# Queries sent with the head dimension outermost, and every other input sent tile by tile

## The chip, the cores and the metric

The kernel runs on one core of one Trainium2 chip. What is measured is the time of the whole program on the device, in microseconds (us); a kernel's time is the median of its runs. The layout in which inputs lie in device memory when the program starts is part of the kernel's own code: it prepares them on the host, and that is not in the time.

## The reference

Three stages follow each other on 8 x 576 = 4608 tokens with 512 features (8 heads of 64).

```python
kv  = einsum('bhsd,bhse->bhde', k, v)          # linear attention, 8 batches, 8 heads
out = einsum('bhsd,bhde->bhse', q, kv)
out = out / sqrt(mean(out*out, -1) + 1e-6) * g_norm
x   = out.transpose(0, 2, 1, 3).reshape(4608, 512)
xn  = x / sqrt(mean(x*x, -1) + 1e-6) * rms_g   # gated feed-forward, width 1536
g   = xn @ w_gate
x   = (g * sigmoid(g) * (xn @ w_val)) @ w_out
e   = argmax(x @ moe2_w_gate, 1)               # one of 8 experts for each token, width 1024
y   = gate * (relu(x @ w1[e]) @ w2[e])         # gate: softmax value of the chosen expert
```

q, k, v, w1 and w2 are float32; w_gate, w_val and w_out come as 64-bit floats, which the kernel narrows itself on ScalarE and VectorE. The large products split each operand in a high and a low part and run three passes.

## The kernel before, in words

The tokens are worked through in nine chunks of 512. A chunk c up to 7 holds 512 tokens of batch c, four to a partition; chunk 8 gathers the last 64 tokens of all eight batches. Chunks 0 to 3 run alone, chunk 4 runs alone with the attention of two batches beside it, and the pairs (4, 5) and (6, 7) run through a form with seven products instead of eight. After chunk 8 come the experts.

TensorE's stream is written by hand. In each chunk a loop over twelve blocks of the feed-forward width issues a gate product (`pg`), a value product (`pv`) and the products with w_out (`po`); between them the function `group` takes at most a step or two from a queue `aux`. The attention of batch c + 1 lies in that queue as a list of steps (`Attention.steps`, lines 797 to 845): between two steps stands an empty one, and the kinds of the steps say at which places of the pairs they are allowed. So an instruction of the attention stands in the stream where its step is taken, and each engine works in the order in which the code issues.

A batch's attention goes by pairs of heads (hp 0 to 3) in two halves of two pairs. `load` brings k, v and q of a pair; `load_left` the last 64 tokens of k and v; `load_last` those of q, two batches together. `column` copies k, and later q, so that the two heads of a pair stand beside each other (lines 679 to 683, on ScalarE; on VectorE for k of batch 0). `kv` multiplies k with v into a block diagonal `kvb`, filled by a copy on VectorE and one on ScalarE (lines 699, 700). `turn` transposes q on TensorE, four transposes for a pair, and ScalarE copies the result out of PSUM (lines 702 to 713). `av` multiplies the turned q with `kvb` and squares the result on ScalarE; GpSimd weighs the squares with g_norm, and VectorE sums both kinds (`squares`, `sums`). `finish`, `root` and `scale` normalise; `tstep` transposes the chunk into `xt`, with `comb` (rms_g times g_norm) as scale.

Batch 0 stands ahead of the loop, written out in lines 1466 to 1516. There 56 transposes of the identity into a tile that nobody reads (line 1505) run between the last `av` and the first `tstep`. The weights of the feed-forward pass through `Convert`: `load`, `rebias` (ScalarE), `narrow` (three passes on VectorE), `high` (ScalarE) and `low` (VectorE), four raw buffers in flight.

All loads named here are issued by SP, in program order; SP waits with a load until its buffer is free. k, v and q have two buffers each, the turned q (tag `qT`) and the column copies (tag `col`) as well.

Of the kernel before, what the change touches and what calls it, by code (L numbers as in the profile page):

```python
# [11 lines left out]
F32 = mybir.dt.float32  # L12
# [54 lines left out]
def attention_moe_kernel(ctx, tc, q, k, v, g_norm, w_gate, w_val, w_out, rms_g, wg2, w1, w2, out):  # L67
# [36 lines left out]
    wg2s = const([P, KD, E], F32, "wg2s")  # L104
    comb = const([P, KD], F32, "comb")
    gcol = const([P, 1], F32, "gcol")
    g2b = const([P, HD], F32, "g2b")
# [18 lines left out]

    def small_loads():
        nc.sync.dma_start(gcol[0:64, :], g_norm.rearrange("(e o) -> e o", o=1))
        nc.sync.dma_start(gcol[64:128, :], g_norm.rearrange("(e o) -> e o", o=1))
        with nc.allow_non_contiguous_dma(reason="one small vector"):  # L130
            nc.sync.dma_start(comb, rms_g.rearrange("(k p) -> p k", p=P))

    def late_loads():
        nc.sync.dma_start(wg2s, wg2.rearrange("(k p) e -> p k e", p=P))
# [39 lines left out]
    class Expert:  # L174
# [12 lines left out]
        def load(self, i):  # L187
            r = raw(f"re{self.nm}_{i}")
            e = self.ereg
            if i < 4:  # L190
                nc.sync.dma_start(
                    r.rearrange("p (k f) -> p k f", k=KD),
                    w1[ds(e, 1), :, i * 256 : i * 256 + 256].rearrange(
                        "o (k p) f -> p (o k) f", p=P
                    ),
                )
            else:
                a = (i - 4) * 256
                nc.sync.dma_start(
                    r.rearrange("p (a d) -> p a d", a=2),  # L200
                    w2[ds(e, 1), a : a + 256, :].rearrange("o (a p) d -> p (o a) d", p=P),
                )
            self.raws[i] = r
# [404 lines left out]
    wgt = dpool.tile([E, D], F32, name="wgt")  # L608
# [12 lines left out]
    class Attention:  # L621


        def __init__(self, b, ps):
            self.b, self.ps = b, ps
            self.n = 5 if b % 2 == 1 else 4
            self.t, self.col = {}, {}
            self.first, self.later = deque(), deque()
            self.qTs = deque()

        def load(self, *hps):
# [3 lines left out]
            for nm in "kvq":  # L635
                for hp in hps:
                    t = att.tile([P, 2, 4, HD], F32, tag=nm, bufs=2, name=f"{nm}{b}_{hp}")
                    nc.sync.dma_start(
                        t.rearrange("p h j d -> p h (j d)"),
                        {"k": k, "v": v, "q": q}[nm][b, 2 * hp : 2 * hp + 2, 0:512, :].rearrange(  # L640
                            "h (p j) d -> p h (j d)", j=4
                        ),
# [7 lines left out]
        def load_rest(self):  # L650

            self.t[2], self.t[3] = {}, {}
            for nm, src in (("k", k), ("v", v), ("q", q)):
                t = wpool.tile([P, 1024], F32R, tag="w", bufs=NSLOT, name=f"{nm}rest").bitcast(F32)
                nc.sync.dma_start(
                    t.rearrange("p (h d) -> p h d", h=4),
                    src[0, 4:8, 0:512, :].rearrange("h (p j) d -> p h (j d)", j=4),
                )
                t = t.rearrange("p (c h j d) -> p c h j d", c=2, h=2, j=4)
                self.t[2][nm], self.t[3][nm] = t[:, 0], t[:, 1]  # L660

        def load_left(self):
# [4 lines left out]
            for dst, src in ((self.kl, k), (self.vl, v)):  # L667
                nc.sync.dma_start(
                    dst[lo : lo + 64], src[b, :, 512:S, :].rearrange("h s d -> s h d")
                )  # L670

        def load_last(self):
            for i in range(2):
                nc.sync.dma_start(
                    x5[64 * i : 64 * i + 64],
                    q[self.b - 1 + i, :, 512:S, :].rearrange("h s d -> s h d"),
                )

        def column(self, nm, hp, copy=nc.scalar.copy):

# [1542 lines left out]
```

## Time and profile before

| | us |
|---|---|
| time, median of 3 runs (1451.55 to 1452.9) | 1452.2 |
| the profiled execution's own time | 1451.66 |
| its span, first to last instruction | 1450.0 |
| TensorE busy (98% of the span) | 1420.8 |
| VectorE busy (64%) | 929.1 |
| ScalarE busy (43%) | 629.3 |
| GpSimd busy (14%) | 197.3 |

The profile is of one execution. Engines are named PE (TensorE's matmuls), PEld (its weight loads, which overlap the matmuls), DVE (VectorE), ACT (ScalarE), POOL (GpSimd) and SPq (SP's issue of DMAs). A matmul of float32 stands in the rows as several passes. Rows give the line of the kernel, the operation and `out<-in` by the tiles' names; a duration of a matmul is its latency, which overlaps that of its neighbours. The granted clock of TensorE was 0.999 of full speed over the execution. Rows of SPq show when a load is issued, not when it lands; a landing is seen where an engine waited for it.

### The profile page before, as it was taken

How to read it: one execution, taken by the hardware profiler on the slowest of the kernel's cores; microseconds unless marked ns; L12 is line 12 of the kernel's file. 1: busy time of each engine (PE TensorE's matmuls, PEld its weight loads, DVE VectorE, ACT ScalarE, POOL GpSimd, SP SyncE). 2: the span in 40 equal slices, each digit the busy share in tenths (PEclk: the TensorE clock that was granted, in tenths of full speed). 3: DMA queues.
4: the chain of work that ended last, by engine and by line, in shares of the span. 5: the costliest groups of instructions: out<-in, count | busy, mean ns of one | idle time of the engine just before them, and what ended most of it. 6: DMA issues, size and time to landing. Idle time of an engine off the chain costs nothing. (4 is left out here: it accounts for less than half of the span.)

```text
span 1450.0 us, 21584 instructions
## 1 busy us (share of the span) xinstructions
PE 1420.8 (98%) x7844; PEld 1195.0 (82%) x7844; DVE 929.1 (64%) x1971; ACT 629.3 (43%) x1173; POOL 197.3 (14%) x207
## 2 busy tenths in 40 slices
PE   6999999999999999999999999999999999999998
PEld 5776788888888878887888888788999989988986
DVE  5989674785677555665657447854362777678672
ACT  5655443333444543444232322243343556556652
POOL 2010001011012010101000100112313212212111
PEclk9999999999999999999999999999999999999999
DMA  8776856665666686559656565764322344334320
GB/s 226 249 221 212 272 168 177 214 224 146 209 214 184 195 262 203 161 176 277 241 193 210 175 202 189 228 208 131 124 89 89 98 138 135 114 122 139 108 92 34
DMA packets 162860, 255.55 MB, mean 176 GB/s; under 512 B 27331, under 2 KB 93123, under 8 KB 162752
## 3 DMA queue, kind: packets, MB, share of 16 engines
q1 hardware_dynamic: 131264, 190.26, 41.6%
q10 hardware_dynamic: 23040, 44.05, 9.5%
q0 software_dynamic: 8448, 19.85, 4.3%
q8 instruction: 63, 1.03, 0.3%
q14 instruction: 45, 0.37, 0.1%
HBM read 199.68 MB, written 55.30 MB: 176 GB/s over the span
## 5 line engine op out<-in xcount | busy, mean ns | idle before, releaser
L1030 DVE SCALAR_TENSOR_TENSOR junk<-x,wgb 128x512 bf16<-128x512 f32 x256 | 183.1, 715 | 5.0
L155 PE MATMUL po<-wo,ahl 128*128 128x512 f32 x408 | 161.0, 395 | 0.9 <-DVE x L1008 0.9
L156 PE MATMUL po<-wo,ahl 128*128 128x512 f32 x408 | 159.1, 390 | 0.0
L157 PE MATMUL po<-wo,ahl 128*128 128x512 f32 x408 | 159.0, 390 | 0.0
L1265 PE MATMUL A<-xp,r 128*128 128x512 f32 x504 | 130.3, 394 | 1.9 <-DVE X L1841 1.3
L1265 PEld LDWEIGHTS A<-xp,r 128*128 128x128 f32 x504 | 93.1, 188 | 22.5 <-DVE X L1841 2.2
L744 POOL TENSOR_TENSOR sg<-sq,g2b 128x512 f32<-128x512 f32 x36 | 48.9, 1359 | 422.9 <-ACT sq L726 350.3
L1103 POOL DMA_INDIRECT idxd<-rec,si x36 | 37.7, 1047 | 457.1 <-DVE cs L1112 344.6
L1265 PE MATMUL X<-xp,r 128*128 128x512 f32 x360 | 93.3, 394 | 1.1 <-ACT X L1832 1.1
L155 PEld LDWEIGHTS po<-wo,ahl 128*128 128x128 f32 x408 | 76.6, 188 | 17.2 <-DVE x L1008 1.4
L157 PEld LDWEIGHTS po<-wo,ahl 128*128 128x128 f32 x408 | 76.6, 188 | 16.3
L156 PEld LDWEIGHTS po<-wo,ahl 128*128 128x128 f32 x408 | 76.7, 188 | 15.3
L1265 PEld LDWEIGHTS X<-xp,r 128*128 128x128 f32 x360 | 66.4, 188 | 15.7 <-ACT X L1832 1.8
L155 PE MATMUL pg<-x,wg 128*128 128x512 f32 x192 | 77.1, 402 | 0.1
L155 PE MATMUL pv<-x,wv 128*128 128x512 f32 x192 | 76.9, 400 | 0.4 <-DVE sl L1902 0.4
L156 PE MATMUL pg<-x,wg 128*128 128x512 f32 x192 | 75.1, 391 | 2.0 <-DVE wg L966 2.0
L156 PE MATMUL pv<-x,wv 128*128 128x512 f32 x192 | 75.4, 393 | 1.3 <-DVE wv L966 1.3
L157 PE MATMUL pg<-x,wg 128*128 128x512 f32 x192 | 75.1, 391 | 0.9 <-DVE x L856 0.9
L157 PE MATMUL pv<-x,wv 128*128 128x512 f32 x192 | 75.0, 391 | 0.0
L1903 ACT ACTIVATE ahl<-sl 128x512 fp32r<-128x512 f32 x42 | 26.5, 631 | 103.1 <-DVE sl L1902 103.1
L252 ACT ACTIVATE wo<-re 128x512 fp32r<-128x512 f32 x84 | 51.1, 626 | 31.8 <-DVE re L263 31.2
L255 DVE TENSOR_TENSOR wo<-re,wo 128x512 fp32r<-128x512 f32 x84 | 56.5, 685 | 9.5 <-ACT wo L252 9.1
(815 smaller groups left out, 3374.1 us busy)
## 6 DMA issues: line engine op xcount, KB each, us to landing
wo<-wos SPq DMA_DIRECT2D x90, 512.0 KB
r<-wst ACTq DMA_DIRECT2D x72, 512.0 KB
re<-in_moe_w SPq DMA_DIRECT2D x64, 512.0 KB
x1d<-x SPq DMA_DIRECT2D x32, 256.0 KB
k<-in_k SPq DMA_DIRECT2D x30, 256.0 KB
v<-in_v SPq DMA_DIRECT2D x30, 256.0 KB
q<-in_q SPq DMA_DIRECT2D x30, 256.0 KB
rg<-in_moe_w_gate SPq DMA_DIRECT2D x12, 512.0 KB
```

The lines of the kernel that those rows point to most:

```text
L155: nc.tensor.matmul(ps, lhi, rhi, start=first, stop=False)
L156: nc.tensor.matmul(ps, llo, rhi, start=False, stop=False)
L157: nc.tensor.matmul(ps, lhi, rlo, start=False, stop=last)
L252: nc.scalar.activation(w[:, 0], part(n), AF.Copy)
L255: nc.vector.tensor_tensor(w[:, 1], part(n), w[:, 0].bitcast(F32), op=ALU.subtract)
L744: nc.gpsimd.tensor_tensor(sg, sq3, g2b[:, None, :].to_broadcast([P, 8, HD]), op=ALU.mult)
L1030: nc.vector.scalar_tensor_tensor(j, self.rows[t], 1.0, wgb[e], op0=ALU.mult, op1=ALU.mult, accum_out=self.L[:, t, e : e + 1],)
L1103: nc.gpsimd.indirect_dma_start(out=idxd[:], out_offset=bass.IndirectOffsetOnAxis(ap=si[:, j : j + 1], axis=0), in_=rec[:, j, :], in_offset ...
L1265: nc.tensor.matmul(ps, w[:, a, kk, :], x[kk][b], start=first and kk == j == 0, stop=kk == 1 and j == 2, skip_group_check=True,)
L1903: nc.scalar.activation(ahl[:, 0:512], sl, AF.Copy)
```

## The change

The host sends every input in the order in which a tile takes it (`laid_out`): one run of memory for each partition. q comes with the head dimension outermost, so that a loaded tile has a pair's 2 x 64 dimensions on the partitions and 4 x 128 tokens beside, which is what `turn` made. With it go `turn`, `column` and `gate_turn` (the transposed gate weights of the experts are sent). k and v keep the head as a further index in the tile, and `kv` reads them there. The four small vectors are one load.

A batch's steps become kv, av, kv, av (and av of the last tokens in odd batches), each with an empty step behind it; `sums` moves from `turn` to the head of a kv step. q of pairs 2 and 3 takes the buffers of the former column copies; a last tile of q takes those of the turned q.

In the start of the program the order is new: the first gate weights are loaded behind the first pair, and their conversion stands between the pairs; two weight loads move behind the loads of batch 1; 12 transposes of the identity stand ahead of the first kv.

```diff
+    smalls = const([P, 112], F32, "smalls")
+    wg2s = smalls[:, 0:32].rearrange("p (k e) -> p k e", e=E)
+    comb, gcol, g2b = smalls[:, 32:36], smalls[:, 40:41], smalls[:, 48:112]
...
         def load(self, i):
             r = raw(f"re{self.nm}_{i}")
             e = self.ereg
+            w, i4 = (w1, i) if i < 4 else (w2, i - 4)
+            nc.sync.dma_start(r, w[ds(e, 1), i4].rearrange("o p n -> p (o n)"))
...
             for nm in "kvq":
                 for hp in hps:
-                    t = att.tile([P, 2, 4, HD], F32, tag=nm, bufs=2, name=f"{nm}{b}_{hp}")
+                    tag = "col" if nm == "q" and hp > 1 else nm
+                    t = att.tile([P, 4, P], F32, tag=tag, bufs=2, name=f"{nm}{b}_{hp}")
                     nc.sync.dma_start(
-                        t.rearrange("p h j d -> p h (j d)"),
-                        {"k": k, "v": v, "q": q}[nm][b, 2 * hp : 2 * hp + 2, 0:512, :].rearrange(
-                            "h (p j) d -> p h (j d)", j=4
-                        ),
+                        t.rearrange("p a b -> p (a b)"), {"k": k, "v": v, "q": q}[nm][b, hp]
                     )
...
-                nc.sync.dma_start(
-                    dst[lo : lo + 64], src[b, :, 512:S, :].rearrange("h s d -> s h d")
-                )
+                nc.sync.dma_start(dst[lo : lo + 64].rearrange("s h d -> s (h d)"), src[b])
...
         def load_last(self):
+            t = att.tile([P, 4, P], F32, tag="qT", bufs=2, name=f"ql{self.b}")
+            nc.sync.dma_start(t.rearrange("p a b -> p (a b)"), ql[self.b // 2])
+            self.t[4] = {"q": t}
...
             def kv(h):
+                self.sums()
                 self.kv(h, h + 1)
-                for hp in (h, h + 1):
-                    self.column("q", hp)
...
-            def turn(h):
-                for hp in (h, h + 1):
-                    self.turn(hp)
-                for hp in (0, 1):
-                    if h == 0:
-                        self.column("k", hp + 2)
-                    elif nxt:
-                        nxt.column("k", hp)
...
             for h in (0, 2):
-                for f, kind in ((kv, "p"), (turn, "p"), (av, "a")):
+                for f, kind in ((kv, "p"), (av, "a")):
...
             if self.n == 5:
-                res += [mark("p", lambda: self.turn(4)), idle]
-                res += [mark("a", lambda: self.av(4, tight)), idle]
+                res += [mark("a", last), idle]
...
     a0.load(0)
+    nc.sync.dma_start(smalls, vectors)
+    conv.load()
     a0.load(1)
-    nc.sync.dma_start(g2b, g_norm.rearrange("(o e) -> o e", o=1).to_broadcast([P, HD]))
     a0.load_rest()
     conv.load()
...
+    unread = otile("unread")
+    for i in range(12):
+        nc.tensor.transpose(unread[:, 0:P], ident, ident)
+    a0.kv(0)
+    nc.vector.tensor_tensor(g2b, g2b, g2b, op=ALU.mult)
+    a0.av(0, True)
+    conv.rebias()
+    a0.squares()
+    conv.narrow()
+    a0.kv(1)
+    a0.later.popleft()()
+    a0.av(1, True)
+    conv.high()
+    a0.kv(2)
+    a0.kv(3)
+    a0.squares()
+    conv.low()
+    a0.av(2, True)
+    a0.sums()
+    a0.av(3, True)
     a1.load(0, 1)
+    conv.load()
+    conv.load()
+    a0.squares()
     conv.rebias()
...
-        aux.extend([gate_turn, fills])
+        aux.append(fills)
```

How the order on three engines changes is shown by the instructions as they are issued; line numbers of the changed kernel are its own (666 and 677 are `kv` and `av`, 703 the sums, 667 the copy of `kvb` on VectorE, 842 the weight loads, 618 and 633 those of q, k, v).

TensorE at the start of the program, from the first pair on; numbers behind a name tell tiles apart, `x8` counts instructions. Before:

```order
L698 MATMUL kv_0_172<-vlast,klast 64x64 x2
L710 MATMUL qT_0_185<-ident,qc_0_170 128x128 x4
L698 MATMUL kv_1_197<-v_1_146,kc_1_192 64x64 x8
L698 MATMUL kv_1_197<-vlast,klast 64x64 x2
L710 MATMUL qT_1_210<-ident,qc_1_195 128x128 x4
L722 MATMUL av_0_219<-kvb_87,qTs_0_190 128x128 x4
```

Now:

```order
L1419 MATMUL unread<-ident 128x128 x12
L666 MATMUL kv_0_170<-v_0_133,k_0_131 64x64 x8
L666 MATMUL kv_0_170<-vlast,klast 64x64 x2
L677 MATMUL av_0_184<-kvb_87,q_0_138 128x128 x4
L666 MATMUL kv_1_200<-v_1_145,k_1_143 64x64 x8
L666 MATMUL kv_1_200<-vlast,klast 64x64 x2
L677 MATMUL av_1_214<-kvb_87,q_1_147 128x128 x4
```

The transposes qT are gone, av of a pair follows its own kv, and twelve transposes that nobody reads stand in front.

SP at the start: `rg` are gate weights, `rv` value weights, `klast` and `vlast` the last tokens, `krest` and so on pairs 2 and 3. Before:

```order
L638 DMA q_0_142<-in_q 128x2x256
L638 DMA k_1_144<-in_k 128x2x256
L638 DMA v_1_146<-in_v 128x2x256
L638 DMA q_1_148<-in_q 128x2x256
L1479 DMA g2b<-in_g_norm 128x64
L655 DMA krest<-in_k 128x4x256
L655 DMA vrest<-in_v 128x4x256
L655 DMA qrest<-in_q 128x4x256
L895 DMA rg_157<-in_moe_w_gate 128x4x256
```

Now:

```order
L618 DMA q_0_138<-in_q 128x512
L1412 DMA smalls<-in_vectors 128x112
L842 DMA rg_141<-in_moe_w_gate 128x1024
L618 DMA k_1_143<-in_k 128x512
L618 DMA v_1_145<-in_v 128x512
L618 DMA q_1_147<-in_q 128x512
L633 DMA krest<-in_k 128x2x512
L633 DMA vrest<-in_v 128x2x512
L633 DMA qrest<-in_q 128x2x512
L842 DMA rv_155<-in_moe_w_val 128x1024
```

The first gate weights moved from behind `qrest` to a place ahead of pair 1.

VectorE in the second half of batch 4: `sq` are squares, `sg` weighed squares, `junk` the logits of an earlier chunk. Before:

```order
L748 TENSOR_REDUCE s_125<-sq_1_3690 128x4x2
L1902 TENSOR_TENSOR sl_1_3672<-sl_1_3672,pv_1_3700 128x512
L1906 TENSOR_TENSOR ahl_1_3713<-sl_1_3672,ahl_1_3713 128x512
L1030 SCALAR_TENSOR_TENSOR junk_0_6_3717,L_3570<-x_2_0_3543,wgb_1478 128x512
L1030 SCALAR_TENSOR_TENSOR junk_0_7_3719,L_3570<-x_2_0_3543,wgb_1478 128x512
L699 COPY kvb_87<-kv_2_3721 64x2x64
```

Now:

```order
L703 TENSOR_REDUCE s_122<-sq_1_3469 128x4x2
L974 SCALAR_TENSOR_TENSOR junk_0_4_3494,L_3393<-x_2_0_3366,wgb_1374 128x512
L974 SCALAR_TENSOR_TENSOR junk_0_5_3496,L_3393<-x_2_0_3366,wgb_1374 128x512
L703 TENSOR_REDUCE s_123<-sg_0_3459 128x4x2
L703 TENSOR_REDUCE s_123<-sg_1_3470 128x4x2
L667 COPY kvb_87<-kv_2_3500 64x2x64
```

The sums of the weighed squares moved ahead of the copy of kv, and the step itself one product forward.

## Rows read from the trace of the kernel before

**Rows 1.** Page, part 1: busy us, share of the span, instructions.

```profile
PE 1420.8 (98%) x7844; PEld 1195.0 (82%) x7844; DVE 929.1 (64%) x1971; ACT 629.3 (43%) x1173; POOL 197.3 (14%) x207
```

**Rows 2.** Stages: us, busy us by engine, granted clock, DMA share, GB/s.

```profile
0.00:20.00 20.00, 9.86 (x109) 8.44 (x109) 4.92 (x13) 8.34 (x17) 5.41 (x14) 1.00 0.89 263
200.00:400.00 200.00, 199.24 (x1111) 165.00 (x1110) 136.17 (x304) 78.29 (x134) 20.34 (x18) 1.00 0.60 185
```

**Rows 3.** Tile qT: count, duration ns (min/median/max), first and last start.

```profile
L710 PE MATMUL qT<-ident,qc x128: 270/273/477, 8.8 to 586.0; 128*128 128x128 f32 x128
...
L710 PE MATMUL qT<-ident,xo x16: 270/272/273, 91.8 to 595.1; 128*128 128x128 f32 x16
```

**Rows 4.** Timeline of TensorE in batch 7: start us, duration us, instruction.

```profile
585.25 1.03 PE L710 MATMUL qT<-ident,qc 128*128 128x128 f32 x8
586.04 1.64 PE L1265 MATMUL X<-xp,r 128*128 128x512 f32 x6
587.52 1.52 PE L1265 MATMUL A<-xp,r 128*128 128x512 f32 x6
...
596.60 1.52 PE L1265 MATMUL X<-xp,r 128*128 128x512 f32 x6
597.96 1.52 PE L1265 MATMUL A<-xp,r 128*128 128x512 f32 x6
```

**Rows 5.** Timeline of the start, engines mixed; in brackets idle time and its releaser.

```profile
4.70 1.12 PE L698 MATMUL kv<-v,kc 128*64 128x64 f32 x16 [4.70 <-DMA v<-in_v]
...
7.65 0.48 PE L698 MATMUL kv<-vlast,klast 128*64 128x64 f32 x4 [1.83 <-DMA vlast<-in_v]
...
8.74 0.21 ACT L700 COPY kvb<-kv 64x64 f32<-64x64 f32 x1
...
11.99 1.91 PE L722 MATMUL av<-kvb,qTs 128*128 128x128 f32 x8
...
13.95 0.60 ACT L726 ACTIVATE sq<-av 128x512 f32<-128x512 f32 x1 [1.12 <-PE av L722]
14.44 0.58 ACT L727 COPY xo<-av 128x512 f32<-128x512 f32 x1
...
16.06 0.62 ACT L682 COPY qc<-qrest 128x512 f32<-128x512 f32 x1 [1.04 <-DMA qrest<-in_q]
...
17.23 1.06 PE L722 MATMUL av<-kvb,qTs 128*128 128x128 f32 x8
...
20.16 0.68 ACT L916 ACTIVATE cmg<-rg 128x512 f32<-128x512 f32 x1
...
20.95 0.42 DVE L929 TENSOR_SCALAR cmg<-cmg 128x512 int32<-128x512 int32 x1
...
22.13 0.69 DVE L933 SCALAR_TENSOR_TENSOR cmg<-rg,cmg 128x512 int32<-128x512 int32 x1
...
22.51 6.28 PE L1506 MATMUL unread<-ident 128*128 128x128 f32 x56
...
23.67 0.64 ACT L956 ACTIVATE wg<-cmg 128x512 fp32r<-128x512 f32 x1
...
29.03 1.32 PE L851 MATMUL xT<-ident,xo 128*128 128x128 f32 x8 [0.25 <-DVE xo L784]
```

**Rows 6.** Waits, three stretches (300-450, 100-150, 30-105): us in total, times, longest.

```profile
PE qT L710 <- ACT qc L682: 0.7, 2, 0.4
...
PE pv L156 <- DVE wv L966: 1.3, 2, 0.7
...
ACT cmw L916 <- DMA rw<-in_moe_w_out: 3.5, 1, 3.5
```

**Rows 7.** Timeline of batch 5 at 418-437: kv on TensorE, v loads on SP.

```profile
422.69 0.69 PE L698 MATMUL kv<-v,kc 128*64 128x64 f32 x16
...
425.18 0.93 SPq L638 DMA_DIRECT2D v<-in_v  x2
...
435.11 0.69 PE L698 MATMUL kv<-v,kc 128*64 128x64 f32 x16
```

More of the change, by code (lines that the diff above doesn't have):

```diff
@@ L66, in attention_moe_kernel @@
 @with_exitstack
-def attention_moe_kernel(ctx, tc, q, k, v, g_norm, w_gate, w_val, w_out, rms_g, wg2, w1, w2, out):
+def attention_moe_kernel(
+    ctx, tc, q, k, v, ql, kl, vl, vectors, w_gate, w_val, w_out, wgt, w1, w2, out
+):
     nc = tc.nc
@@ L125, in late_constants @@
         nc.gpsimd.memset(acc, 0.0)
[L127 to L134, printed above, removed]
     live = [0]
@@ L607, in attention_moe_kernel @@
     xt = [None] * KD
-    wgt = dpool.tile([E, D], F32, name="wgt")
     wgb = []
@@ L689, in kv @@
             for c, hp in enumerate(hps):
-                kc = self.col["k", hp]
+                kt, vt = (
+                    self.t[hp][nm].rearrange("p a (i d) -> p (a i) d", i=2) for nm in "kv"
+                )
                 for j in range(5):
@@ L700, in kv @@
             nc.scalar.copy(kb[64:128, h0 : h0 + n, 64:128], pt[64:128, 0:n, 64:128])
-        def turn(self, hp):
-            self.sums()
-            ps = self.ps(f"qT{self.b}_{hp}")
-            for j in range(4):
-                if hp < 4:
-                    src = self.col["q", hp][:, j, :]
-                else:
-                    src = x5[:, 2 * j : 2 * j + 2, :].rearrange("p h d -> p (h d)")
-                nc.tensor.transpose(ps[:, j * P : j * P + P], src, ident)
-            qT = att.tile([P, 4, P], F32, tag="qT", bufs=2, name=f"qTs{self.b}_{hp}")
-            nc.scalar.copy(qT.rearrange("p a b -> p (a b)"), ps)
-            self.qTs.append(qT)
         def av(self, hp, apart=False):
-            b, kb, qT = self.b, kvb[self.b % 2], self.qTs.popleft()
+            b, kb, qT = self.b, kvb[self.b % 2], self.t[hp]["q"]
             ps = self.ps(f"av{b}_{hp}")
@@ L893, in load @@
             else:
[L894 to L898 removed]
+                nc.sync.dma_start(r, (w_gate if kind == "g" else w_val)[f])
             self.raws.append(r)
@@ L1455, in overflow_plan @@
         nc.vector.tensor_copy(ovs, oe)
-    def gate_turn():
-        ps = ptile("wgt")
-        for kk in range(KD):
-            nc.tensor.transpose(ps[0:E, kk * P : kk * P + P], wg2s[:, kk, :], ident)
-        ws = att.tile([E, D], F32, tag="tmp", bufs=3, name="wgts")
-        nc.scalar.copy(ws, ps[0:E, :])
-        nc.sync.dma_start(wgt[:], ws)
     warm = const([P, 1], F32, "warm")
@@ L1477, in attention_moe_kernel @@
     a0.load(0)
+    nc.sync.dma_start(smalls, vectors)
+    conv.load()
     a0.load(1)
-    nc.sync.dma_start(g2b, g_norm.rearrange("(o e) -> o e", o=1).to_broadcast([P, HD]))
     a0.load_rest()
     conv.load()
-    small_loads()
-    for _ in range(3):
-        conv.load()
-    for hp in range(4):
-        a0.column("k", hp, vec)
-        if hp == 1:
-            nc.vector.tensor_tensor(g2b, g2b, g2b, op=ALU.mult)
-        if hp > 1:
-            a0.av(hp - 2)
-        a0.column("q", hp)
-        a0.kv(hp)
-        if hp == 3:
-            conv.rebias()
-        a0.turn(hp)
-    a1.load(0, 1)
-    late_loads()
-    conv.narrow()
-    a0.av(2)
-    a0.av(3)
-    conv.high()
+    unread = otile("unread")
[18 more added lines that the diff above has]
+    a0.av(3, True)
+    a1.load(0, 1)
+    conv.load()
+    conv.load()
+    a0.squares()
     conv.rebias()
@@ L1508, in attention_moe_kernel @@
     nc.vector.tensor_scalar(comb, comb, gcol[:, 0:1], None, op0=ALU.mult)
-    conv.low()
     a0.root()
     nc.scalar.activation(warm, warm, AF.Silu)
-    for kk in range(KD):
-        a0.scale(kk)
+    a0.scale(0)
+    a0.scale(1)
+    a0.scale(2)
     tstep(0, 0)
+    a0.scale(3)
     tstep(0, 1)
```

86 lines of the change are left out of this document (43 added, 43 removed).

## Prediction

> **What bounds the kernel now.** I read the page's first part before anything else: TensorE is busy 98% of the span, VectorE 64%, ScalarE 43% [rows 1]. So where TensorE works without gaps, time goes only if TensorE's own work goes, or if one of its few gaps closes. The table by stage says where the gaps are: in the first 20 us TensorE is busy 9.86 us, between 200 and 400 us 199.24 of 200 [rows 2]. That makes two regimes. The start is a chain from the first loads through ScalarE and VectorE to the first projection; after it TensorE is the limit and each pass costs its own pitch. Attention lies in both: batch 0 in the start, batches 1 to 7 as steps between the matmuls of the projections up to about 600 us (the last turn starts at 595.1 [rows 3]), after which the change touches only the shape of expert weight loads.
>
> **The turns.** The tile qT is written by 128 transposes from the column copies and 16 from the four last tiles [rows 3]; with four for the gate weights (line 1460) 148 go. Sixteen are batch 0's and lie in the start, which is reckoned below. In the stream 112 + 16 + 4 = 132 are left.
>
> What is one worth there? The duration in [rows 3], 272 ns, is a latency and overlaps its neighbours, so I take starts. In batch 7 a step of eight begins at 585.25 and the next product at 586.04: 0.79. That product's six passes then take 1.48 to the next start, where an undisturbed six take 1.36 (596.60 to 597.96): 0.12 more for the change of shape [rows 4]. So 0.91 us for eight. The dummy transposes before the first projection give the same pitch: 56 in 6.28 us, 112 ns each [rows 5]. Seven batches with two steps: 14 x 0.91 = 12.7. Five steps of four (the last tiles and the gate) at half that, 0.46: 2.3. **Sum 15.0 us**, on the path because TensorE has no gaps there. Between the step's 114 ns for each and the latency of 272 the start times are what the stream loses, so I keep the former.
>
> The Trainium skill ("TensorE: Matmul & The Clock Gate", Back-to-back issue gap) gives about 81 ns for each matmul of 128 columns in a stream with its weight loads. By that the 132 would be an estimated 10.7 us, and the forecast 4.3 us later, at 1435.9; the rows are of these very instructions and say 112 to 114 ns, so the measurement decides.
>
> **The copies.** ScalarE loses, in steady state, two column copies and an eviction for each pair of heads. At 43% busy it is no bound, so I count these at nothing, with two exceptions. Twice between 300 and 450 us a turn waited for its column copy, 0.7 us in total [rows 6]; those waits have no object any more: **-0.7**. In the first chunk VectorE, which splits the projection weights, makes TensorE wait 1.3 us between 100 and 150 us [rows 6], as the far end of a ScalarE that stood 3.5 us before a w_out load; that load was queued behind a burst of q, k, v and last-row loads. The bytes stay, but the last rows come in one piece per row instead of eight pieces of 256 bytes. I take **-0.3** from this. Its bounds: -1.3 (all of the wait goes) and +2.7 (the first chunk is paced by VectorE after all, and batch 1's share of the turns, two steps of eight, one of four and the gate's, 2 x 0.91 + 2 x 0.46 = 2.7, comes back as waits).
>
> **The start.** Before: k and v of the first pair are there at 4.70, but the last rows of v at 7.65; the mask copies end at 8.95 (8.74 + 0.21); the first projection's transposes start at 29.03, and the dummies ahead of them at 22.51 [rows 5]. The dummies begin as the last av drains, so 6.4 us lie between that end and 29.03: the dummies' 6.28, and beside them the last sums, the normalisation and the first scaling. That stretch is the same in both kernels, except that a weight subtraction leaves it and a third temporary tile can hold a square back; I keep 6.4.
>
> After: in front of the last rows stand the same k and v, so the rest is their own 0.26 MB. At the rate of the first 20 us, 263 GB/s [rows 2], these take 1.0 us: last rows at 5.7. Then, each item with its row in [rows 5]:
> - tail of kv and both copies, 7.65 to 8.95: 1.3, so 7.0;
> - av of pair 0, 1.91 and 0.05 to its square: 9.0 (no turn stands between);
> - square and copy, 13.95 to 15.02: 1.1, then the first touch of the gate weights, 0.68: 10.8;
> - three VectorE passes on these weights, 20.95 to 22.82: 1.9, so 12.7; kv of pair 1 is done, but its copy stands behind these passes: 0.5, so 13.2;
> - av of pair 1 at the quick pace, 1.06: 14.2; square, copy and the high half of the weights, 1.1 + 0.64: 16.0; two small copies 0.4: 16.4;
> - av of pairs 2 and 3, 2 x 1.06: 18.5; plus 6.4: **24.9**.
>
> q of pairs 2 and 3 must be there at 16.4. It came at 16.06 before [rows 5]; now 0.52 MB of weights stand ahead of it, 2.0 us at the same rate, against the 1.95 us saved at the last rows. I take 16.1, just not the limit. So the first projection starts at 24.9 instead of 29.03: **-4.1**. Behind it VectorE does the same work in nearly the same order, so the shift should carry. Bounds: -2 (q two us late) and -6.5 (all of this a third quicker).
>
> I took the slow av for pair 0: eight passes take 1.91 us at 12 us and 1.06 at 17 us [rows 5], the ratio of TensorE's two levels (1.2 and 2.4 GHz), though the granted clock of the whole stretch is given as 1.00 [rows 2]. If the 12 new dummies at the very start bring the quick pace forward, it is 24.1 instead of 24.9; no row shows transposes alone from the start, so I keep 1.91.
>
> **New waits.** Three things get tighter. First, k, v of pairs 2 and 3: their tiles are now given back by kv alone, and kv of the second half comes one product and one turn sooner. The narrowest place is batch 5: kv starts at 422.69, its v loads are out by 426.11, and kv of the second half starts at 435.11 [rows 7]. Without the turn (0.91) and one product of twelve passes (2 x 1.36 = 2.7) that is 431.5: 5.4 us for a landing. Queued on TensorE behind a late one is the whole projection. I cost it at 0; the last rows of batch 0, 2.9 us behind their neighbour, and the late w_out load say that a wait of 1 to 2 us is possible, at four places (batches 4 to 7), so up to +6. Second, the sums of the squares now stand on VectorE ahead of the copy of kv: two more instructions over 512 elements, 1.4 us if each takes the 0.69 of [rows 5], in front of a copy that av needs one product later; VectorE reaches them before kv ends, so 0, at worst +1 at two places. Third, SP: the q loads no longer wait for a column copy, which can only help.
>
> **Sum.** 15.0 + 0.7 + 0.3 + 4.1 = 20.1. The profiled execution took 1451.66 us (span 1450.0), 0.5 below the median of 1452.2; 1451.66 - 20.1 = **1431.6 us**; a median may lie that half microsecond higher, which the range holds.
>
> **Rivals.**
> - *The start does not move*: a load behind the reordered weights is late, or the chain behind 24.9 is VectorE's and waits there. For it: the start's sum is a chain of ten items, q arrives within 1 us of its need. Against: the order on TensorE shows that the turns and copies are gone from it. Time 1451.7 - 15.0 - 0.7 = 1436, with 1434 to 1438.
> - *The stream gives back*: VectorE paces the first chunk (+2.7) and loads are late at the four close steps (up to +6). For it: VectorE was the last that TensorE waited for there [rows 6]. Against: ScalarE and the queues get lighter at the same places. 1435 to 1440, 1437 as its centre.
> - *More than the sum*: all of the wait of [rows 6] and 6.5 us at the start: 1451.7 - 15.0 - 0.7 - 1.3 - 6.5 = 1428, down to 1426.
> - *Slower*: the loads of the second half arrive after their kv at the four close steps, because k is no longer freed by an early copy. To eat 20.1 us each must wait 5.0, that is, land 10.4 us after its issue. From there on it is slower: 1453 at 10.8. Against: nothing in these rows is that late; the last rows of v, in their 256 byte pieces, were there 7.65 us after the program began [rows 5].
>
> **How the numbers follow.** My forecast 0.60 (its own range 1428 to 1435), start not moved 0.16, stream gives back 0.13, more than the sum 0.07, slower 0.04. The range takes the first with half of its neighbours: 1426.5 to 1438.5; beyond it lie the slow end of the second rival and the last. A measurement of this kernel tells 0.2% (3 us) from no change; faster than that are all cases but the last and a mishap or two: 0.95, within 0.02, slower 0.03.
>
> **What would show it.** TensorE's busy time falls by about 15 us and qT is gone from its rows; the first transposes of xT start at 24 to 25.5 us, the dummies before them at about 18.5, with av of pair 0 still at 1.9 us; eight fewer transposes shorten a chunk's step by 0.9; no wait of a kv for a load of k or v in batches 4 to 7; the wait for the split weights between 100 and 140 us does not grow. The prediction is wrong if xT starts after 27, if waits for VectorE in the first chunk exceed 4 us, or if a kv of the second half waits for a DMA.

## The result, and the profile after

The changed kernel takes 1438.9 us (median; 1436.1 to 1441.0), the kernel before on the same chip 1451.9 us (1451.3 to 1452.9): a ratio of 0.991 (95% interval 0.989 to 0.993). Forecast were 1431.6 us with a range of 1426.5 to 1438.5. The direction is right, the gain is 13 us instead of 20, and the time lies just outside the range.

One sentence above, on the attention beside each chunk, is wrong: chunks 0 to 2 have one batch's attention beside them (batches 1, 2 and 3), chunk 3 that of batches 4 and 5, and the pair (4, 5) that of 6 and 7. The prediction's count of steps is not touched by it.

The page's first part of the changed kernel answers to [rows 1]:

```profile
PE 1409.2 (98%) x7708; PEld 1183.8 (82%) x7708; DVE 930.6 (65%) x1967; ACT 579.0 (40%) x1076; POOL 200.7 (14%) x207
```

TensorE's busy time fell by 11.6 us, to 1409.2; the span fell by 10.9, to 1439.1. The two stages of [rows 2]:

```profile
0.00:20.00 20.00, 13.73 (x126) 12.17 (x127) 5.59 (x14) 6.35 (x14) 5.81 (x15) 1.00 0.91 306
200.00:400.00 200.00, 196.48 (x1078) 161.96 (x1077) 137.08 (x297) 62.95 (x108) 22.95 (x19) 1.00 0.61 195
```

In the second, TensorE was busy 199.24 us before and is busy 196.48 now: in a stretch that had 0.8 us of gaps there are now 3.5. The gain has to be looked for stretch by stretch. The table cuts each profiled execution at the same instructions of TensorE (the first xT transposes of chunks 0 to 3, the first X product of the pairs, the first gate product of chunk 8), all starts taken from TensorE's timeline; the last column is the median of the runs. What follows, chunk 8 and the experts, takes 600.6 us of the span before and 600.8 after; in the later profiles it takes 598.3 to 600.1, so a profiled time can differ by 2 us for a reason that lies outside the stretches.

| kernel | first xT at | chunk 0 | chunk 1 | chunk 2 | chunk 3 | pairs | time |
|---|---|---|---|---|---|---|---|
| before | 29.03 | 116.04 | 110.77 | 110.41 | 126.04 | 357.07 | 1451.9 |
| change forecast | -4.1 | -3.0 | -1.8 | -2.3 | -4.8 | -4.1 | -20.1 |
| after | 26.56 | 116.82 | 107.59 | 111.87 | 122.57 | 352.97 | 1438.9 |
| after_again | 26.19 | 115.20 | 107.60 | 111.98 | 122.58 | 356.80 | 1439.2 |
| e1_fills_late | 27.44 | 112.66 | 107.59 | 111.11 | 122.57 | 353.63 | 1436.4 |
| e2_before_fills_early | 28.97 | 118.30 | 109.56 | 110.46 | 126.10 | 356.51 | 1452.9 |
| e3_spaced | 26.26 | 112.10 | 108.39 | 108.14 | 120.60 | 354.35 | 1431.9 |
| e4_turns_back | 28.15 | 115.70 | 109.35 | 112.19 | 124.06 | 357.16 | 1446.9 |
| e5_sums_behind_kv | 26.75 | 112.67 | 107.59 | 112.03 | 120.54 | 351.99 | 1433.2 |
| e6_v1_first | 26.98 | 111.85 | 108.81 | 108.12 | 120.61 | 353.66 | 1430.4 |
| e7_v1_first_warm | 28.01 | 112.51 | 107.86 | 108.12 | 120.61 | 353.58 | 1431.1 |
| e8_batch3_late | 26.54 | 112.66 | 107.59 | 108.33 | 122.58 | 353.54 | 1431.3 |
| e9_three_mends | 27.87 | 112.67 | 107.60 | 108.11 | 120.54 | 354.27 | 1430.7 |
| e10_mends_rest_first | 26.16 | 112.70 | 107.60 | 108.11 | 120.54 | 352.83 | 1428.5 |
| e11_fills_on_pool | 26.68 | 112.63 | 107.59 | 111.82 | 122.57 | 353.23 | 1437.3 |
| e12_loads_two_steps_on | 26.81 | 117.44 | 107.59 | 108.13 | 122.56 | 353.33 | 1435.7 |
| e13_all_mends | 26.71 | 117.72 | 107.59 | 108.13 | 120.91 | 352.65 | 1433.9 |

The forecast's row is the prediction's sum laid on the stretches: 2 x 0.91 + 2 x 0.46 + 0.3 in chunk 0, 2 x 0.91 in chunk 1, 0.46 more in chunk 2, 4 x 0.91 + 0.46 + 0.7 in chunk 3, 4 x 0.91 + 0.46 in the pairs. Chunk 3 of after is 3.5 us shorter (4.8 forecast) and its pairs 4.1. Chunk 1 gains 1.4 us more than forecast. Three places give back: chunk 0 is 0.8 us longer instead of 3.0 shorter, chunk 2 is 1.5 longer instead of 2.3 shorter, and the start gains 2.5 instead of 4.1.

**The start**, TensorE's timeline of the changed kernel with two rows of VectorE (start us, duration us, instruction, idle time and its releaser), against [rows 5]:

```profile
1.56 2.82 PE L1419 MATMUL unread<-ident 128*128 128x128 f32 x12 [1.56 <-POOL ident masks.py:199]
...
6.56 0.48 PE L666 MATMUL kv<-vlast,klast 128*64 128x64 f32 x4 [1.04 <-DMA vlast<-in_v_last]
7.67 2.08 PE L677 MATMUL av<-kvb,q 128*128 128x128 f32 x8 [0.62 <-ACT kvb L668]
11.13 1.12 PE L666 MATMUL kv<-v,k 128*64 128x64 f32 x16 [1.39 <-DMA v<-in_v]
...
12.84 0.69 DVE L877 SCALAR_TENSOR_TENSOR cmg<-rg,cmg 128x512 int32<-128x512 int32 x1
13.45 0.21 DVE L667 COPY kvb<-kv 64x64 f32<-64x64 f32 x1
...
13.95 2.08 PE L677 MATMUL av<-kvb,q 128*128 128x128 f32 x8 [1.48 <-ACT kvb L668]
15.96 1.12 PE L666 MATMUL kv<-vrest,krest 128*64 128x64 f32 x16
...
17.96 2.05 PE L677 MATMUL av<-kvb,qrest 128*128 128x128 f32 x16 [0.16 <-ACT kvb L668]
19.85 6.28 PE L1445 MATMUL unread<-ident 128*128 128x128 f32 x56
26.56 1.32 PE L799 MATMUL xT<-ident,xo 128*128 128x128 f32 x8 [0.43 <-DVE xo L739]
```

The last rows of v arrive 0.9 us later than the 5.7 reckoned, and av of pair 1 takes 2.08 us, not the 1.06 taken for it. So the dummies begin at 19.85 instead of 18.5; from there to xT it is 6.7 us. The kv of pair 1 waits 1.39 us for its v, until 11.13, but that costs nothing here: the copy of its result stands behind VectorE's three passes on the first weights, the last of which ends at 13.53.

**Chunk 0**, rows of SyncE (SP in the text above), ScalarE, VectorE and TensorE of the changed kernel in order of time:

```profile
118.98 0.33 SPq L842 DMA_DIRECT2D rg<-in_moe_w_gate  x1
119.40 0.86 SPq L1477 DMA_DIRECT2D idxd<-bigt  x2
...
120.35 5.47 SPq L1483 DMA_DIRECT2D x1d<-zt  x8
...
127.29 1.17 SPq L842 DMA_DIRECT2D rv<-in_moe_w_val  x1
...
133.17 0.66 ACT L860 ACTIVATE cmv<-rv 128x512 f32<-128x512 f32 x1 [6.42 <-DMA rv<-in_moe_w_val]
...
133.86 0.43 DVE L873 TENSOR_SCALAR cmv<-cmv 128x512 int32<-128x512 int32 x1 [4.19 <-ACT cmv L860]
...
134.89 0.50 PE L147 MATMUL pg<-x,wg 128*128 128x512 f32 x1 [0.89 <-ACT wg L900]
...
136.40 0.76 PE L148 MATMUL pg<-x,wg 128*128 128x512 f32 x1 [1.01 <-DVE wg L910]
```

SyncE spends 6.4 us on the ten stores of `fills` (119.40 to 125.8), and rv, a load of split weights for one of the last blocks, is issued at 127.29. ScalarE stands 6.42 us for it, VectorE 4.19 behind ScalarE, TensorE behind both. Before, those stores stood behind all these loads: the queue `aux` has seven steps less in chunk 0, so `fills`, its last step, is taken earlier.

The two waits of TensorE, 0.89 and 1.01 us, are not all that this costs. Behind them the clock granted to TensorE falls to 0.50, which is the lower of its two levels (1.2 GHz). The first row is that stretch, in the columns of [rows 2]; then come two passes of TensorE in it:

```profile
136.47:139.88 3.41, 3.41 (x8) 2.71 (x9) 3.31 (x7) 0.81 (x2) 0.00 (x0) 0.50 0.13 50
...
138.24 0.63 PE L149 MATMUL pg<-x,wg 128*128 128x512 f32 x1
138.67 0.63 PE L147 MATMUL pg<-x,wg 128*128 128x512 f32 x1
```

The same two passes in after_again, a second profile of the same kernel, where the waits are 0.69 and 1.01 us and the granted clock stays at 1.00:

```profile
136.80 0.39 PE L149 MATMUL pg<-x,wg 128*128 128x512 f32 x1
137.03 0.40 PE L147 MATMUL pg<-x,wg 128*128 128x512 f32 x1
```

One pass starts 0.43 us behind the other at the lower level and 0.23 at the upper. Half of 3.41 us, an estimated 1.7 us, is what the lower level costs, and chunk 0 of the two profiles differs by 1.6 us.

**Chunk 2**, the waits of TensorE and one of SyncE (total, times, longest), and behind them SyncE's timeline and VectorE's:

```profile
PE pv L147 <- DVE sl L1842: 1.9, 2, 1.3
PE av L689 <- ACT xo L682: 0.8, 1, 0.8
...
SPq L618 <- PE kv L666: 9.0, 4, 6.2
```

```profile
268.81 0.87 SPq L648 DMA_DIRECT2D ql<-in_q_last  x1
275.97 0.91 SPq L618 DMA_DIRECT2D k<-in_k  x2
...
282.71 0.43 SPq L1134 DMA_DIRECT2D wst<-tm  x1
...
286.17 0.82 SPq L1108 DMA_DIRECT2D wst<-wv  x1
```

```profile
286.81 1.29 DVE L1115 TENSOR_TENSOR tm<-wv 128x512 f32<-128x512 f32 x2 [4.28 <-DMA wst<-tm]
288.02 0.68 DVE L1842 TENSOR_TENSOR sl<-sl,pv 128x512 f32<-128x512 f32 x1
```

In the kernel before, TensorE has no gap in this chunk. Now SyncE issues the last q tile, ql, at 268.81 and then nothing until 275.97: the next load is k of the next batch, and its buffer is one that the kv of this very step still has to read. Before, ScalarE's column copy had emptied it early, and SyncE waited 1.3 us for kv in the whole stretch. Behind that load stand the stores of the split terms (wst), out at 281 to 287; VectorE waits 4.28 us, until 286.81, for a buffer that a store still reads, and is then late with sl, for which TensorE waits 1.33 us at 301 and 0.57 at 318.

### The profile page after: what moved, and what is told of

It reads as the page before. It is cut to its first block, busy times and chain, and to the rows that moved or that the text cites. A ratio compares the mean times of both kernels' runs of the same rounds, so it can differ in the third digit from the quotient of the medians.

```text
span 1439.1 us, 21164 instructions
## 1 busy us (share of the span) xinstructions
PE 1409.2 (98%) x7708; PEld 1183.8 (82%) x7708; DVE 930.6 (65%) x1967; ACT 579.0 (40%) x1076; POOL 200.7 (14%) x207
## 3 DMA queue, kind: packets, MB, share of 16 engines
q0 software_dynamic: 8448, 19.85, 4.2%
## 5 line engine op out<-in xcount | busy, mean ns | idle before, releaser
L974 DVE SCALAR_TENSOR_TENSOR junk<-x,wgb 128x512 bf16<-128x512 f32 x256 | 186.8, 730 | 5.1 <-ACT x L950 0.2
L699 POOL TENSOR_TENSOR sg<-sq,smalls 128x512 f32<-128x512 f32 x36 | 48.8, 1357 | 363.0 <-ACT sq L681 306.3
```

Source lines behind the costliest of these rows:

```text
L699: nc.gpsimd.tensor_tensor(sg, sq3, g2b[:, None, :].to_broadcast([P, 8, HD]), op=ALU.mult)
L974: nc.vector.scalar_tensor_tensor(j, self.rows[t], 1.0, wgb[e], op0=ALU.mult, op1=ALU.mult, accum_out=self.L[:, t, e : e + 1],)
```

## The experiments

Each time is the median of 4 to 11 executions, with the kernel before run beside them; the medians and stretches are in the table.

**The fills.** e1 takes `aux.append(fills)` out and calls `fills()` behind the chunk's last loads; e2 puts them early in the kernel before; e11 leaves them early in the changed kernel, but lets GpSimd issue them (both `dma_start` in `fills`).

```diff
e1     -            aux.append(fills)
...
       +                    fills()
                            gate_loads()
e2     -            aux.extend([gate_turn, fills])
       +            aux.append(gate_turn)
       +            aux.insert(24, fills)
e11    -            nc.sync.dma_start(
       +            nc.gpsimd.dma_start(
```

> The changed kernel with the ten stores of the fills issued behind the last split-weight loads of chunk 0, where they stood before the change; nothing else differs. Theory (the stores hold up SyncE's queue, so that the weights of the last two blocks land about 6 us later and ScalarE, VectorE and TensorE run dry at 127 to 140 us): chunk 0, from the first xT to the xT of chunk 1, shrinks from 116.8 to 113.0-114.2 us, ScalarE's 6.42 us wait for rv falls under 2 us, time 1435.5 us (1434.5 to 1437). Rival (VectorE is busy nearly all the time from 45 to 127 us and paces chunk 0 anyway): the wait moves to VectorE, chunk 0 stays within 0.7 us of 116.8, time 1438.5.

> The kernel before, with its fills issued ten queue entries earlier, in front of the last three split-weight loads, as they stand in the changed kernel. Theory (the stores alone cost the time): chunk 0 grows from 116.0 to about 118.5-119.5 us and the time from 1451.9 to 1455 us (1454 to 1456). Rival (only the changed kernel, with VectorE full, feels it): no change, 1451 to 1453.

> The changed kernel with the fills at their early place, but their ten stores issued by GpSimd instead of SyncE. Theory (what costs is that the loads of the last split weights stand behind the stores in SyncE's queue): the loads of rv and rw are issued 5 to 7 us earlier and chunk 0 falls from 116.8 to 112.5-113.5 us as in e1, time 1436 us. Rival (the stores themselves slow the loads, or VectorE shares something with them): chunk 0 stays above 115.5 us, time 1438 to 1440.

e1: chunk 0 falls by 4.2 us to 112.66, a bit below what was expected; 1436.4 us (ratio to before 0.990, 0.9885 to 0.9915). Of the 4.2 us, 1.9 are idle time of TensorE (5.5 us in chunk 0 of the changed kernel, 3.6 in e1) and an estimated 1.7 the stretch at the lower clock. Against after_again, which has no such stretch in chunk 0, it is 2.5 us, and e1's median lies 2.5 and 2.8 us below the two medians of the changed kernel. The rival, that VectorE paces the chunk anyway, is out.

e2: chunk 0 of the kernel before grows by 2.3 us, of which 0.6 are idle time and an estimated 1.7 a stretch with the granted clock at 0.50 (140.70 to 144.12 us). But chunk 1, at whose head the stores had stood, shrinks by 1.2; the total moves less than can be told (ratio 1.001, 1.000 to 1.002), and the 1455 us expected did not come. Where the 1.2 us come from is not shown: 0.37 of them were a wait for sl at 211.7, over 60 us behind the stores, and in e1, where the stores are late again, chunk 1 is 107.59 as in the changed kernel.

e11 separates the queue from the stores: same place in the program, same bytes, another issuer, and chunk 0 is 112.63; 1437.3 us. SyncE of e11 in that stretch:

```profile
119.04 0.33 SPq L842 DMA_DIRECT2D rg<-in_moe_w_gate  x1
...
121.42 0.33 SPq L842 DMA_DIRECT2D rv<-in_moe_w_val  x1
```

rv is issued at 121.42 instead of 127.29. GpSimd comes to the stores earlier than SyncE did, at 83.1 to 89.6 us, so their traffic has moved too; but from its issue to its use by ScalarE rv takes 5.6 us in e11 (until 127.02) and 5.9 in the changed kernel (until 133.17), both with ScalarE waiting. So it is the late issue that costs, not a slower transfer: SyncE's queue. (The Trainium skill, "DMA: Bandwidth & Descriptors", Issuing engines are not separate DMA queues, says that another issuer saves only the time of issuing, usually small beside the transfer. Here that time alone was 6.4 us for ten stores, and a chunk lost 2.5 to 4.2 us to it.)

**Chunk 2 and chunk 3.** e3 is e1 with two empty steps where each turn stood; e8 is e1 with six empty steps ahead of batch 3's steps; e5 is e1 with the sums behind kv; e12 is e1 with the loads of the kv step moved to the av step behind it (`loads` takes over what stood in `kv`).

```diff
e3     +                    if kind == "p":
       +                        res += [idle, idle]
...
       -                res += [mark("a", last), idle]
       +                res += [idle, idle, mark("a", last), idle]
e8     +            if self.b == 3:
       +                res += [idle] * 6
e5     -                self.sums()
                        self.kv(h, h + 1)
       +                self.sums()
e12    +            def loads(h):
...
                    def av(h):
       +                if h < 4:
       +                    loads(h)
```

> The kernel of e1_fills_late with two empty steps put where each turn step stood, so that the steps of a batch keep the distances that they had before the change. Theory (steps that follow closer bunch VectorE's sums, squares and logits, and so cost 3.7 us in chunk 2 and about 1.5 us at two kvb copies in chunk 3): chunk 2 falls from 111.9 to 108.2-109.5 us, the wait of TensorE for sl near 301 us goes, time 3 to 5 us below e1, about 1431.5 us. Rival (the backlog in chunk 2 comes from the logits and the split terms and not from the distances): chunk 2 stays at 111 to 112 us, time within 1 us of e1.

> The kernel of e1_fills_late with six empty steps ahead of batch 3's steps in chunk 2, whose distances stay close. Theory A (what costs in chunk 2 is that the reductions follow one another closely): chunk 2 stays at 110.5 to 111.2 us. Theory B (what costs is that all of batch 3's steps now lie in the first 16 groups, in which VectorE also has two logits each, instead of ending behind them): the waits for sl go and chunk 2 falls to 108.2-109 us, time 1434 us.

> The kernel of e1_fills_late with the sums of an earlier pair issued behind the kv step and its kvb copies instead of ahead of them. Theory (the two waits of TensorE for kvb in chunk 3, 1.5 us together, are the reductions that stand ahead of the copy on VectorE, 1.3 us of them at a time): both waits go, chunk 3 falls from 122.6 to 121.0-121.4 us, chunk 2 stays at 111.1, time 1435 us against 1436.4 of e1. Rival (the copy waits for something else on VectorE, such as logits or conversions): chunk 3 stays within 0.4 us.

> The kernel of e1_fills_late with the loads of a batch's later tiles issued by the av step instead of the kv step ahead of it, two groups further on in SyncE's order; the steps and their distances stay as in e1. Theory (in chunk 2 SyncE stands 6.2 us at a load of k that waits until the kv of the same step has read the buffer, the stores of the split terms stand behind it, VectorE then stands 4.3 us for a buffer that such a store still reads, and comes late to sl): SyncE's waits for kv in chunk 2 fall from 9.0 us to under 3, VectorE's wait for the stores goes, TensorE's 1.9 us wait for sl goes, chunk 2 falls from 111.1 to 108.1-108.6 us. Rival (VectorE's backlog is the coincidence of the reductions with the logits, whatever SyncE does): chunk 2 stays above 110 us. Chunk 0 112.7, chunk 1 107.6 either way; time 1433 to 1434.5 by the theory, 1436 by the rival.

e3: chunk 2 108.14 and chunk 3 120.60, no wait of TensorE left in either; 1431.9 us (ratio 0.987, 0.985 to 0.989), the time that the prediction gave, though not by its terms: the start and the pairs gain less than forecast, chunks 0, 1 and 3 more. e8: chunk 2 108.33, 1431.3 us, below the 1434 expected. Its expectation had this as proof that the logits and the reductions must not coincide (theory B). That was too quick: shifting the steps also takes the stores of the split terms out from behind the load of k, as e3 does (SyncE's waits for kv in chunk 2 are 9.0 us in the changed kernel, 2.5 in e3, 0.4 in e8). e12 moves nothing but the loads in SyncE's order: these waits are 0.6 us and chunk 2 is 108.13, where e1, e5, e11 and the two profiles of the changed kernel have 111.1 to 112.0. VectorE's wait for the stores in that chunk is down from 4.3 to

```profile
DVE tm L1119 <- DMA wst<-tu: 1.0, 1, 1.0
```

and TensorE waits for nothing there. Distances and coincidence are as in e1, so neither makes the wait by itself; SyncE's queue does, a second time.

e5 names the two waits in chunk 3. First the changed kernel at the first of them, then VectorE of e5 at the same place:

```profile
384.98 1.27 DVE L703 TENSOR_REDUCE s<-sg 128x8 f32<-128x512 f32 x2
...
386.17 0.27 DVE L667 COPY kvb<-kv 64x128 f32<-64x128 f32 x1
386.47 0.26 ACT L668 COPY kvb<-kv 64x128 f32<-64x128 f32 x1 [4.09 <-DVE kvb L667]
...
386.79 1.38 PE L677 MATMUL av<-kvb,q 128*128 128x128 f32 x10 [0.77 <-ACT kvb L668]
```

```profile
381.17 0.28 DVE L667 COPY kvb<-kv 64x128 f32<-64x128 f32 x1
381.37 1.26 DVE L703 TENSOR_REDUCE s<-sg 128x8 f32<-128x512 f32 x2
```

In the changed kernel two sums (1.27 us) stand on VectorE ahead of the copy of kv, ScalarE's half follows it, and av waits 0.77 us (and 0.71 at 426.24). In e5 the copy goes first: both waits are gone and chunk 3 falls by 2.0 us to 120.54, a bit more than expected; 1433.2 us.

e12 has a price elsewhere, which was not expected: its chunk 0 is 117.44, and its time 1435.7 us. The loads for the second half of batch 1 now go out some 7 us later, and kv of that half waits for v:

```profile
59.35 0.90 SPq L618 DMA_DIRECT2D v<-in_v  x2
...
64.83 0.69 PE L666 MATMUL kv<-v,k 128*64 128x64 f32 x16 [3.12 <-DMA v<-in_v]
```

Issued from 59.35 on, the two v tiles are there at 64.83, 5.5 us later. Behind this wait of 3.12 us the granted clock is 0.50 from 65.81 to 69.22 us, an estimated 1.7 us more; together these are the 4.8 us by which chunk 0 is above e1's. It is the wait of the prediction's "slower" rival, brought about by the edit, in a batch that the rival did not name.

**The price of a turn.** e4 puts four transposes of the identity ahead of the av of each pair of batches 1 to 7.

```diff
e4     +                if b > 0:
       +                    for j in range(4):
       +                        nc.tensor.transpose(ps[:, j * P : j * P + P], ident, ident)
```

> The changed kernel with four transposes of the identity put ahead of the av matmuls of each pair of batches 1 to 7 (28 pairs, 112 transposes; their result is overwritten). It prices the removed turns in the stream. Theory (TensorE is the bound, each removed step of eight was worth its busy time of 0.91 us): 14 x 0.91 = 12.7 us more, spread as 1.8 per batch and 3.6 per period of two batches, time 1451.5 us (1449.5 to 1453). Rival (part of the turns lay in time that TensorE would have waited anyway): 8 us or less, time under 1447.5 us.

1446.9 us against 1438.9 and 1439.2: 8 us, not 12.7, as its rival had it. In chunk 1, where TensorE waits for nothing, 16 transposes cost 1.76 us, 110 ns each, as forecast. (The 81 ns of the Trainium skill, "TensorE: Matmul & The Clock Gate", Back-to-back issue gap, would give an estimated 1.3.) In chunk 2 they cost 0.2 to 0.3 and in chunk 3 1.5 instead of 3.6, because they fill time that the changed kernel waits away; the kvb waits of chunk 3 are gone in e4.

**The start.** e6 is e3 with pair 1 loaded ahead of the first split weights and their conversion behind kv 3; e7 adds dummies (18 instead of 12 in front, 4, 6 and 4 ahead of av 0, kv 1 and av 1); e10, on top of e9, loads pairs 1, 2 and 3 ahead of the first split weights and moves their conversion behind kv 3 and the last av.

```diff
e6     -    conv.load()
            a0.load(1)
       +    conv.load()
            a0.load_rest()
e10    -    conv.load()
            a0.load(1)
            a0.load_rest()
       +    conv.load()
            conv.load()
```

> The kernel of e3_spaced with k, v and q of pair 1 loaded ahead of the first split weights, and the conversion of those weights moved behind the kv steps on VectorE and behind the last av on ScalarE. Theory (the second pair waits for its v and then for the kvb copy behind the narrowing, 1.4 and 1.5 us in the changed kernel's trace): TensorE waits less than 0.6 us for v of pair 1 and 0.7 us for kvb, the last av ends 1.5 to 3 us earlier and the first xT starts at 24 to 25.3 us instead of 26.3 to 28.2, time 1429.5 to 1431. Rival (the later loads, krest, vrest and qrest, or TensorE's low clock set the end of the av steps): xT within 0.7 us of 26.3 to 27.5, time as e3.

> The kernel of e6_v1_first with 18 instead of 12 transposes of the identity ahead of the first kv, and 4, 6 and 4 of them into the same PSUM tiles ahead of av 0, kv 1 and av 1. Theory (av 0, kv 1, av 1 and kv 2 run at the low pace, 2.08 us for eight passes instead of 1.1, because TensorE has idled between them): from kv 1 on the passes run at the quick pace, xT 1 to 2 us earlier than in e6, 23 to 24.5 us. Rival (the pace at the start is not set by these gaps): the added transposes cost 0.24 us each where nothing is waited for, xT 0.5 to 1.5 us later than in e6.

By xT, at 26.98 and 28.01, e6 and e7 fall to their rivals; e6's time, 1430.4 us, lies in the range of its theory, but its interval overlaps that of e3. In e6 v of pair 1 is there at 9.17 and av 1 starts at 11.06, 2.9 us earlier than in the changed kernel and 1.6 earlier than in e3, but then kv 2 waits 1.68 us for vrest, at 14.81, and the last two av take 2.86 us at the slow pace: the wait has moved on to the next load. In e7 av of pair 0 is quick (1.16 us), but so it is in e3 and e6 with 12 dummies (the changed kernel has 2.08 us in one profile and 1.50 in the other), and from av of pair 1 on (2.07 us) the pace is slow again.

**Together.** e9 has the fills of e1, the sums of e5 and the empty steps of e8; e13 is e10 with e12's loads in place of the empty steps.

> The changed kernel with three mends at once: the fills behind the last split weights of chunk 0, the sums behind the kv step, and six empty steps ahead of batch 3's steps. If the causes are separate, the stretches add up as they came out one by one: chunk 0 112.7 us, chunk 1 107.6, chunk 2 108.1-108.4, chunk 3 120.5, pairs 347.8-349, together 797-798 us from the first xT to the last X product against 807.6 of the changed kernel; with a start at 26.3 to 28 us the time is 1427.5 to 1430. If they share a cause (VectorE's backlog is only pushed on), at least one stretch is 1 us or more above these.

> The kernel of e9_three_mends with the first loads in the order pair 0, small vectors, pair 1, pairs 2 and 3, and only then the first split weights, whose conversion is moved behind kv 3 and av 3. Theory (kv 2 starts when vrest has landed, 14.8 us with the first split weights ahead of it, and they are 0.5 MB, 1.3 us at 400 GB/s): kv 2 starts at 13.3 to 13.8 us, first xT at 25 to 26 us, time 1 us below e9. Rival (TensorE's slow pace and the chain of sums set the end): kv 2 starts earlier and xT stays at 26.3 to 27.5 us, time as e9; a product that waits for the first split weights would show as a wait of TensorE for wg near 28 us.

> The kernel of e10_mends_rest_first with the six empty steps taken out and the loads issued by the av step as in e12 instead. If that mends chunk 2 by itself, the stretches are 112.7, 107.6, 108.1-108.6, 120.5 and 348 to 350 us and the time 1427.5 to 1430, as e10; if the empty steps did something else, chunk 2 is above 110 us and the time 1430 to 1432.

> The changed kernel once more, unaltered, for the spread from one profiled execution to the next: the stretches chunk 0 to chunk 3 are expected within 0.3 us of 116.8, 107.6, 111.9 and 122.6, the start (first xT 26.56) within 1.5 us, the stretch behind the last X product within 2 us, the time 1437 to 1440.5.

(The expectations of e9 and e13 end the pairs at the last X product, 4.2 us ahead of the table's cut.) In e9 the mends add up in chunks 0 to 3. The time, 1430.7 us, is just above the 1427.5 to 1430 expected: the profile has a late start (27.87) and, in the pairs, a wait of 2.00 us for a split-term load (A for r<-wst) that is 0.77 in the changed kernel. e10 brings kv 2 to 13.76 and the dummies to 18.49:

```profile
13.76 1.12 PE L666 MATMUL kv<-vrest,krest 128*64 128x64 f32 x16
...
18.49 6.28 PE L1447 MATMUL unread<-ident 128*128 128x128 f32 x56
26.16 1.32 PE L801 MATMUL xT<-ident,xo 128*128 128x128 f32 x8 [1.39 <-DVE xo L739]
```

xT now waits 1.39 us for VectorE, which has the conversion in its chain, so both the theory and the rival are half right. e10 is the best version here: 1428.5 us, ratio to before 0.985 (0.983 to 0.986), 0.7% below the changed kernel. e13 carries e12's price in chunk 0 (117.72) and so misses its 1427.5 to 1430: 1433.9 us. after_again repeats chunks 1 to 3 to 0.1 us; chunk 0, the start and the pairs vary by 1.6, 0.4 and 3.8 us, the first and the last by more than expected. Chunk 0 is the lower clock of the first profile, shown above. In the pairs 1.2 us are the wait for r, 0.77 us in one and 1.97 in the other, and behind the longer one the granted clock is 0.50 from 509.59 to 516.41 us, which is of the size of the other 2.6 us. Not every such wait brings it: e9 waits 2.00 us for r at the same place and keeps 1.00.

## Why the prediction was wrong

- *The turns, -15.0.* Right in price and count: chunk 1 of e4 gives 110 ns each, qT is gone, and from the first xT to chunk 8 e3 is 16.8 us shorter than before (803.6 against 820.3) and e10 18.6, where 16.0 were forecast. Luck is in these sums: they hold what chunk 1 gained beyond the forecast, 1.4 us, for which nothing here shows a cause. The sign "TensorE's busy time falls by about 15 us" did not come out (11.6): it left out the 12 new transposes, 2.82 us, and passes at the lower clock count as busy for longer.
- *"Third, SP: the q loads no longer wait for a column copy, which can only help."* This is the step that failed. It named what SyncE no longer waits for, and not what now stands ahead of what in its queue. The stores of `fills` passed in front of the last split weights (4.2 us by e1 and e11 in a profile in which the granted clock also fell, 2.5 in one in which it did not), and a load of k that waits for kv passed in front of the stores of the split terms (3.7 us by e12, 111.87 to 108.13; 3.0 against e1). The first of the new waits did see that kv alone now gives k back, but asked only whether the load lands late, not what stands behind it in the queue. The term for the first chunk, -0.3 with a bound of +2.7, saw a wait for VectorE as the danger there; it came as a wait of ScalarE for a load. (The 1.3 us that it read for VectorE between 100 and 150 us are the value weights alone; 0.8 us for the gate weights stand beside them in that stretch of the kernel before.) The sign set for it, waits for VectorE above 4 us, could tell nothing: over chunk 0 they are 4.4 us in the kernel before and 4.8 in the changed one.
- *The sums ahead of the copy of kv, "0, at worst +1 at two places".* The worst came: 0.77 and 0.71; mending it gave 2.0 in chunk 3.
- *The start, -4.1.* The mechanism is right, the size off: -2.5 in this profile, and over ten profiles with the same order of the start xT lies at 26.2 to 28.2. The last rows of v came 0.9 us late, and av of pair 1, for which the sum took the quick pace, ran 1.0 us longer. The bound of -2 held for the profile, not for all.
- *No kv waits for k or v in batches 4 to 7.* Right.
- *The rivals.* "The stream gives back" came nearest in time (1437), with none of its two mechanisms: neither VectorE's own work nor late landings, but the order in one queue.

Chunk 1's extra gain, the spread of the start from run to run, and why the granted clock falls behind some waits and not behind others are not explained.

## What to carry to other kernels

When steps leave a queue that several kinds of work share, list for each queue what now stands in front of what: a step that was not touched can be issued earlier and hold up a load that was in time. A copy that only seems to cost time can be what frees a buffer; without it the next load waits at the head of its queue, and stores that have nothing to do with it wait too. Before pricing this at nothing, follow the first instruction behind each load that will wait, and who needs it. And read the granted clock behind a wait of TensorE before sizing what the wait costs: here a stretch at the lower level cost about as much as the waits ahead of it (1.7 and 1.9 us in chunk 0).

## What the runs showed of the hardware

TensorE's slow pace at the start does not always show in the granted clock of a stage: in the changed kernel eight passes of av take 2.08 us in a stage (0 to 20 us) whose clock is given as 1.00, and in e6 they take the same 2.08 us (11.06 to 13.14) with the clock given as 0.50:

```profile
10.00:15.00 5.00, 2.77 (x22) 2.32 (x21) 0.81 (x2) 1.84 (x4) 1.69 (x2) 0.50 1.04 388
```

Columns: stretch, its length, busy us (instructions) of PE, PEld, DVE, ACT and POOL, granted clock, DMA share, GB/s. The two do not contradict each other. The trace of the changed kernel holds no record of the clock before 17.0 us, that of the kernel before none before 14.4, and time without a record is given as 1.00; e6's records begin at 5.2 us. So the 1.00 that the prediction read there says nothing of the first stage. In e7 the pace fell from quick at av of pair 0 to slow at av of pair 1 with one idle time of 2.27 us, for v, between them; its granted clock falls to 0.50 at 12.73 us.
